# A spectral filter and a gated MLP on one core: the five engines' programs written without the block construct

## The chip, the cores and the metric

The kernel runs on one core of a Trainium2 chip. A core has five engines with an instruction queue each: TensorE (PE, with its weight loads listed as PEld), VectorE (DVE), ScalarE (ACT), GpSimd (POOL) and SyncE (SP, which here only issues transfers and waits). They run side by side and are held together by semaphores: an instruction can wait until a semaphore has reached a value, and raise one when it is done. The metric is the device time of one execution in microseconds (us); a shorter one is better.

## The reference

Layer norm of the input without scale or shift, then the sum of three parts: the input itself, a two-dimensional FFT filter, and a GELU-gated MLP.

```python
xn = _layernorm(x, axis=-1)                      # x: 1 x 2048 x 512, bf16
X  = rfft2(xn) * (w_r + 1j * w_i)                # filter of 2048 x 257
A  = irfft2(X, s=(2048, 512))
h  = gelu(xn @ w_gate) * (xn @ w_up)             # 512 -> 1792
B  = h @ w_down                                  # 1792 -> 512
out = x + A + B
```

## The kernel before, in words

The 2048 rows lie in 16 tiles of 128 rows in SBUF (`x_sb`). Each tile gets its statistics on DVE (`stats`), is normalised (`norm`) and transposed (`turn` on PE for the first ones, `turn_dma` by transposing transfers for the rest) into `xnT`. The MLP runs over four groups of four tiles and 14 chunks of 128 hidden columns: `gated` makes gate and up products in PSUM (`ps_gu`, L707), ACT evacuates them with GELU and a copy, DVE multiplies them into `hT` (L714), and `down` (L759) multiplies by `w_down` and adds the result to `x_sb`. The FFT filter is a chain of folded DFT products on PE (`ps_sp`) with butterflies on DVE between them, spread among the MLP's matmuls. For the last four tiles `down` comes at the very end; each is added on DVE (L770) and stored by a transfer of its own (`store`, L775), the last tile in two parts of 384 and 128 columns. The 17 stores are noted in `sch.finals`.

None of this is issued by hand. Every operation is registered in `_Sched` with its engine, an estimated cost, its reads and writes and a rank. `run` simulates the engines and fixes one order for each of them (`self.order`). `emit` then works out which waits each operation needs (`waits`), gives every engine one semaphore and every transfer one of its own, and writes the programs: `body(e, eng)` goes through one engine's list and, for each operation, issues its waits, the operation, and the increment of its semaphore. For SP it ends with a wait for each of the 17 stores (L327).

The change concerns only how `body` is called. In the kernel before this stands inside `with nc.Block() as block:` (L329), with a decorated function for each engine. The construct lets each engine jump from the common beginning of the program into a body of its own, and at the end lets each jump to a common last part, in which all engines drain their queues and meet: each of the four others reports to POOL on one semaphore, POOL waits for all four and then releases them on another. A wait that `body` asks for is put on the instruction that follows it, or becomes an instruction of its own where one has no room for more.

A meeting of the same kind stands at the beginning of every such program. It belongs to the `Bacc` object made in `kernel` (L1021), together with four small fills of constants on POOL, and lies outside of the construct.

Of the kernel before, what the change touches and what calls it, by code (L numbers as in the profile page):

```python
# [144 lines left out]
class _Sched:  # L145
# [123 lines left out]
    def emit(self, nc, es):  # L269
        sem = {e: es.enter_context(nc.semaphore("sem_" + e)) for e in self.ENGINES}  # L270
        cnt = {e: 0 for e in self.ENGINES}
        val = {}
        for e in self.ENGINES:
            for o in self.order[e]:
                if o.dma:
                    val[o] = (es.enter_context(nc.semaphore("dma%d" % o.seq)), 16, ("dma", o.seq))
                else:
                    cnt[e] += 1
                    val[o] = (sem[e], cnt[e], e)
        know = {}  # L280
        cur = {e: {} for e in self.ENGINES}
        waits = {}
        idx = {e: 0 for e in self.ENGINES}
        done = set()
        progress = True
        while progress:
            progress = False
            for e in self.ENGINES:
                while idx[e] < len(self.order[e]):
                    o = self.order[e][idx[e]]  # L290
                    if any(p not in done for p in o.preds):
                        break
                    need = []
                    c = cur[e]
                    for p in sorted((p for p, w in o.preds.items() if w), key=lambda p: -p.end):
                        s, v, n = val[p]
                        if c.get(n, 0) >= v:
                            continue
                        need.append((s, v, n))
                        for n2, v2 in know[p].items():  # L300
                            if c.get(n2, 0) < v2:
                                c[n2] = v2
                    best = {}
                    for s, v, n in need:
                        if n not in best or best[n][1] < v:
                            best[n] = (s, v)
                    waits[o] = list(best.values())
                    k = dict(c)
                    s, v, n = val[o]
                    k[n] = max(k.get(n, 0), v)  # L310
                    know[o] = k
                    done.add(o)
                    idx[e] += 1
                    progress = True
        assert all(idx[e] == len(self.order[e]) for e in self.ENGINES), "the orders of the engines form a circle"

        def body(e, eng):
            for o in self.order[e]:
                for s, v in waits[o]:
                    eng.wait_ge(s, v)  # L320
                ins = o.fn(eng)
                s, v, n = val[o]
                ins.then_inc(s, 16 if o.dma else 1)
            if e == "sp":
                for o in self.finals:
                    s, v, n = val[o]
                    eng.wait_ge(s, v)  # L327

        with nc.Block() as block:  # L329

            @block.sync
            def _(eng):
                body("sp", eng)

            @block.scalar
            def _(eng):
                body("act", eng)

            @block.vector
            def _(eng):  # L340
                body("dve", eng)

            @block.gpsimd
            def _(eng):
                body("pool", eng)

            @block.tensor
            def _(eng):
                body("pe", eng)


def bass_parallel_sum__spectral_gfnet__glu_gated_geglu__prompt_kernel(
# [683 lines left out]
```

## Time and profile before

| | us |
|---|---|
| median of 3 runs | 170.94 (170.75 to 171.29) |
| profiled execution, its own time | 171.11 |
| its span, first to last instruction of the program | 169.2 |
| PE busy (matmuls) | 165.7, 98% of the span |
| DVE busy | 145.9, 86% |
| ACT busy | 107.5, 64% |
| POOL busy | 10.5, 6% |

The span is counted from the first recorded instruction of the program, the drain of the opening meeting, to the end of its last, the release of the closing one. The execution's own time also holds what lies around the program, here 1.91 us. Instructions that only the sequencer of an engine handles (waits, drains, branches, the issuing of transfers) are marked with a q behind the engine's name and don't count as busy. In the listings by source line a row gives the engine, the operation and how often it ran, then the shortest, median and longest duration in ns, and the starts of the first and the last in us. "issue" is time in which an engine waited for nothing that the profile shows.

### The profile page before, as it was taken

The page shows a single profiled execution, that of the slowest core. Times are in us where ns is not written, and L with a number is a line of the kernel's source. Part 1 is how long each engine was busy: PE and PEld are TensorE (multiplying, and loading weights), DVE is VectorE, ACT ScalarE, POOL GpSimd, SP SyncE. Part 2 cuts the span into 40 slices and gives each one's busy share as a digit, 9 for nine tenths or more (in the row PEclk, how much of TensorE's full clock was granted, in tenths as well). Part 3 has the DMA queues.
Part 4 walks back from the last instruction along what each step waited for, and adds up shares of the span by engine and source line. Part 5 has one row for each costly group of instructions (what it writes and reads, how often), then busy time and mean ns, then how long its engine had stood idle before and what let it go on. Part 6 is the DMA issues. An engine that isn't in the chain of part 4 may idle for free.

```text
span 169.2 us, 2755 instructions
## 1 busy us (share of the span) xinstructions
PE 165.7 (98%) x1019; PEld 88.2 (52%) x1019; DVE 145.9 (86%) x294; ACT 107.5 (64%) x182; POOL 10.5 (6%) x25
## 2 busy tenths in 40 slices
PE   8999999999999999999999999999999999999994
PEld 3688884444554654344444446455444556544443
DVE  2785999997956399999999999999999995999932
ACT  3598887663975966669494739669556499761000
POOL 2030232520000000002000000000000000000000
PEclk9999999999999999999999999999999999999999
DMA  5999999995640625535000000000000000033311
GB/s 147 339 290 182 308 297 99 255 296 101 161 105 10 138 73 103 112 66 187 2 0 0 0 4 0 0 0 4 2 0 0 0 0 4 3 128 117 130 62 62
DMA packets 24927, 16.02 MB, mean 95 GB/s; under 512 B 10957, under 2 KB 24274, under 8 KB 24914
## 3 DMA queue, kind: packets, MB, share of 16 engines
q1 hardware_dynamic: 23714, 15.03, 37.3%
q10 hardware_dynamic: 1200, 0.82, 1.5%
q8 instruction: 8, 0.13, 0.3%
q14 instruction: 5, 0.04, 0.1%
HBM read 11.38 MB, written 2.10 MB: 80 GB/s over the span
## 4 chain that ended last, share of the span: by engine, by line
PE 93%; DMA 4%; DVE 1%; SPq 0%; issue 0%; DVEq 0%
PE ps_gu L707 54%; PE ps_dn L759 21%; PE ps_sp L759 7%; DMA xnT<-specB 2%; PE ps_sp L984 2%; PE ps_sp L615 2%; DMA x_sb<-in_A_x_dram 2%; PE ps_sp L843 2%; PE ps_gu L726 1%; PE ps_sp L924 1%; PE ps_sp L925 1%; PE ps_dn L726 1%; DVE bst L514 0%; PE ps_sp L847 0%; SPq L464 0%
## 5 line engine op out<-in xcount | busy, mean ns | idle before, releaser
L707 PE MATMUL ps_gu<-xnT,wg 128*128 128x512 bf16 (+1 forms) x252 | 57.1, 350 | 0.1
L707 PE MATMUL ps_gu<-xnT,wu 128*128 128x512 bf16 (+1 forms) x252 | 57.1, 350 | 0.0
L713 ACT ACTIVATE uu<-ps_gu 128x512 bf16<-128x512 f32 (+1 forms) x63 | 34.5, 547 | 12.6 <-PE ps_gu L707 11.5
L712 ACT ACTIVATE gg<-ps_gu 128x512 bf16<-128x512 f32 (+1 forms) x63 | 34.4, 550 | 11.3 <-PE ps_gu L707 9.7
L759 PE MATMUL ps_dn<-wd,hT 128*128 128x512 bf16 x168 | 39.2, 379 | 0.0
L707 PEld LDWEIGHTS ps_gu<-xnT,wu 128*128 128x128 bf16 x252 | 24.4, 98 | 21.5 <-ACT gg L712 0.2
L707 PEld LDWEIGHTS ps_gu<-xnT,wg 128*128 128x128 bf16 x252 | 24.3, 98 | 21.2 <-DMA xnT<-specB 0.4
L468 DVE TENSOR_TENSOR specB<-specB 128x512 bf16<-128x512 bf16 (+2 forms) x58 | 33.4, 610 | 0.7 <-ACT specB L989 0.5
L714 DVE TENSOR_TENSOR hT<-gg,uu 128x512 bf16<-128x512 bf16 (+1 forms) x63 | 23.6, 382 | 5.1 <-ACT uu L713 4.8
L759 PEld LDWEIGHTS ps_dn<-wd,hT 128*128 128x128 bf16 x168 | 16.1, 98 | 18.8 <-issue 0.4
L767 ACT ACTIVATE db<-ps_dn 128x512 bf16<-128x512 f32 x12 | 7.2, 597 | 17.5 <-PE ps_dn L759 17.5
L514 DVE BATCH_NORM_STATS2 bst<-x_sb 128x6 f32<-128x512 bf16 x16 | 10.9, 684 | 3.6 <-DMA x_sb<-in_A_x_dram 3.5
L468 DVE TENSOR_TENSOR specC<-specB 128x1024 bf16<-128x1024 bf16 (+2 forms) x18 | 12.6, 714 | 0.3
L759 PE MATMUL ps_sp<-wd,hT 128*128 128x512 bf16 (+2 forms) x70 | 12.3, 336 | 0.0
L468 DVE TENSOR_TENSOR specB<-specA 128x2048 bf16<-128x2048 bf16 x8 | 9.4, 1221 | 2.4 <-ACT specA L620 2.3
L759 PEld LDWEIGHTS ps_sp<-wd,hT 128*128 128x128 bf16 x70 | 6.3, 98 | 6.1 <-DVE x_sb L770 0.2
L468 DVE TENSOR_TENSOR specB<-specB,filt 128x2048 bf16<-128x2048 bf16 x8 | 9.4, 1223 | 0.0
L852 ACT ACTIVATE specA<-ps_sp 128x1024 bf16<-128x1024 f32 x8 | 7.9, 1039 | 1.3 <-PE ps_sp L843 1.3
L620 ACT ACTIVATE specA<-ps_sp 128x1024 bf16<-128x1024 f32 x8 | 7.9, 1029 | 0.3 <-PE ps_sp L615 0.3
L989 ACT ACTIVATE specB<-ps_sp 128x1024 bf16<-128x1024 f32 x8 | 8.0, 1038 | 0.0
L930 ACT ACTIVATE specC<-ps_sp 128x1024 bf16<-128x1024 f32 x8 | 7.8, 1043 | 0.0
L468 DVE TENSOR_TENSOR specA<-specB 128x2048 bf16<-128x2048 bf16 (+1 forms) x8 | 7.6, 986 | 0.1
(68 smaller groups left out, 122.0 us busy)
## 6 DMA issues: line engine op xcount, KB each, us to landing
out_dram<-x_sb SPq DMA_DIRECT2D x15, 128.0 KB, 1.8
wd<-in_B_w_down_dram SPq DMA_DIRECT2D x1, 1792.0 KB, 8.5
x_sb<-in_A_x_dram SPq DMA_DIRECT2D x3, 512.0 KB, 7.3
toki<-c_ti SPq DMA_DIRECT2D x1, 768.0 KB, 4.3
tokf<-c_tf SPq DMA_DIRECT2D x1, 576.0 KB, 4.1
x_sb<-in_A_x_dram SPq DMA_DIRECT2D x4, 128.0 KB, 3.7
wg<-in_B_w_gate_dram SPq DMA_DIRECT2D x2, 256.0 KB, 6.5
wu<-in_B_w_up_dram SPq DMA_DIRECT2D x2, 256.0 KB, 6.4
```

The lines of the kernel that those rows point to most:

```text
L468: return op("dve", c_tt(n), lambda e: e.tensor_tensor(o.ap, a.ap, b.ap, f), reads=(a, b), writes=(o,), key=key, **kw)
L514: op("dve", 0.61, lambda e: e.bn_stats(bst[:, s].ap, xs(s).ap), reads=(xs(s),), writes=(bst[:, s],), key=key, due=due, after=after)
L620: op("act", c_act(1024), lambda e, yv=yv, t=t: e.activation(yv.ap, spair(t).rearrange("p (s r i) -> p s i r", s=4, r=4), ACT.Copy), writes ...
L707: ins = e.matmul(gub(t, n), w.ap[:, dc, fc * P:(fc + 1) * P], xnT.ap[:, b, sl, dc, :], start=(dc == 0), stop=(dc == 3))
L712: op("act", c_act(n), lambda e: e.activation(gg.ap[:, gs.slot, 0:n], gub(g, n), ACT.Gelu_apprx_tanh), tiles=(g, gs), key=0.0)
L713: op("act", c_act(n), lambda e: e.activation(uu.ap[:, us.slot, 0:n], gub(u, n), ACT.Copy), tiles=(u, us), key=0.0)
L714: op("dve", c_tt(n), lambda e: e.tensor_tensor(hT.ap[:, h.slot, lo:lo + n], gg.ap[:, gs.slot, 0:n], uu.ap[:, us.slot, 0:n], MUL), tiles=(g ...
L759: ins = e.matmul(bank(), hT.ap[:, hs[(b, fc)].slot, sl * P:(sl + 1) * P], wd.ap[:, fc, lo:lo + n], start=(fc == 0), stop=(fc == NFC - 1))
L767: op("act", c_act(n), lambda e: e.activation(db.ap[:, d.slot, 0:n], bank(), ACT.Copy), tiles=(t, d), key=0.0)
L852: op("act", c_act(1024), lambda e, xv=xv, t=t: e.activation(xv.ap, spair(t), ACT.Copy), writes=(xv,), tiles=(t,), key=-0.5)
L930: op("act", c_act(1024), lambda e, gv=gv, t=t: e.activation(gv.ap, spair(t).rearrange("p (k x i) -> p k x i", k=4, x=4), ACT.Copy), writes ...
L989: op("act", c_act(1024), lambda e, rv=rv, t=t: e.activation(rv.ap, spair(t), ACT.Copy), writes=(rv,), tiles=(t,), key=-0.5)
```

## The change

The construct is gone. The five calls of `body` stand one after the other at the end of `emit`, each with the engine object itself, so that every engine's instructions go straight into the common stream of the program. No engine gets a body of its own to jump into, and there is no last part with drains and a meeting: each engine's program simply ends after its last instruction, SP's after the wait for the last of the 17 stores. Orders, waits, semaphores and the operations are those of before. The order of the calls (SP, ACT, PE, DVE, POOL) is the order in which the program is written, not one in which the engines run.

```diff
@@ -326,27 +326,8 @@
                     s, v, n = val[o]
                     eng.wait_ge(s, v)
 
-        with nc.Block() as block:
-
-            @block.sync
-            def _(eng):
-                body("sp", eng)
-
-            @block.scalar
-            def _(eng):
-                body("act", eng)
-
-            @block.vector
-            def _(eng):
-                body("dve", eng)
-
-            @block.gpsimd
-            def _(eng):
-                body("pool", eng)
-
-            @block.tensor
-            def _(eng):
-                body("pe", eng)
+        for e, eng in (("sp", nc.sync), ("act", nc.scalar), ("pe", nc.tensor), ("dve", nc.vector), ("pool", nc.gpsimd)):
+            body(e, eng)
```

## The prediction

> **What bounds the kernel now.** I read the page first: the engines' busy times, then the chain of work that ended last.
>
> ```profile
> span 169.2 us, 2755 instructions
> PE 165.7 (98%) x1019; PEld 88.2 (52%) x1019; DVE 145.9 (86%) x294; ACT 107.5 (64%) x182; POOL 10.5 (6%) x25
> ...
> PE 93%; DMA 4%; DVE 1%; SPq 0%; issue 0%; DVEq 0%
> ```
>
> TensorE (PE) is busy in 165.7 of 169.2 us, and 93% of the chain is its matmuls. The change touches no matmul, no transfer and no wait between them, so nearly all of the time is out of its reach. Two places can matter: the few tenths of a microsecond before the first instruction of `body`, and what follows the last matmul. For the second I read the chain of waits in order of time and then the timeline, both from 154 and 166 us on.
>
> ```profile
> 154.83 12.14 PE ps_sp L759 x70
> 166.97 0.02 issue
> 166.99 0.29 DVE x_sb L770
> ```
>
> ```profile
> 166.79 0.85 SPq L775 DMA_DIRECT2D out_dram<-x_sb  x2
> ```
>
> TensorE stops at 166.97. VectorE adds the last 128 columns until 167.28, and SyncE (SP) issues the last two stores, the second until 166.79 + 0.85 = 167.64. From there on only SP has something to wait for: the landing of the stores. Three answers of the trace show that end, line by line: L775 (the stores), L327 (SP's waits for them) and L329, which is the `with nc.Block()` line itself. The last of the three stands complete, with its drains.
>
> ```profile
> L775 SPq DMA_DIRECT2D out_dram<-x_sb x2: 332/332/333, 166.8 to 167.3; - x2
> ...
> DMA to landing us min/median/max: 1.4/1.5/1.6
> ```
>
> ```profile
> L327 SPq EVENT_SEMAPHORE  x8: 28/28/28, 167.7 to 168.8; - x8
> ```
>
> ```profile
> L329 POOLq EVENT_SEMAPHORE  x2: 17/17/17, 169.1 to 169.1; - x2
> L329 POOLq DRAIN  x1: 647/647/647, 79.8 to 79.8; - x1
> L329 ACTq DRAIN  x1: 627/627/627, 154.9 to 154.9; - x1
> L329 PEldq DRAIN  x1: 1622/1622/1622, 165.4 to 165.4; - x1
> L329 DVEq DRAIN  x1: 330/330/330, 167.0 to 167.0; - x1
> L329 SPq COMPARE_BRANCH  x1: 41/41/41, 168.8 to 168.8; - x1
> L329 SPq DRAIN  x1: 13/13/13, 169.0 to 169.0; - x1
> L329 SPq EVENT_SEMAPHORE  x1: 17/17/17, 169.2 to 169.2; - x1
> L329 ACTq EVENT_SEMAPHORE  x1: 17/17/17, 169.2 to 169.2; - x1
> L329 DVEq EVENT_SEMAPHORE  x1: 21/21/21, 169.2 to 169.2; - x1
> L329 PEldq EVENT_SEMAPHORE  x1: 51/51/51, 169.2 to 169.2; - x1
> ```
>
> The columns are shortest, median and longest duration in ns, and the starts of the first and last of the group in us. The last store is issued at 167.3 and lands after 1.4 us, at 168.7. SP's last wait on L327 follows at 168.8. Then comes what the construct itself adds: SP's branch at 168.8, its drain at 169.0, the message from GpSimd (POOL) at 169.1, and the five engines' release at 169.2. The other four engines have drained before 167.4 (167.0 + 0.33 for VectorE is the latest) and wait for SP alone.
>
> **The change, part by part.**
>
> *The meeting at the end* goes: five drains and six semaphore instructions. PE's, ACT's, DVE's and POOL's drains end before 167.4, under the landing of the stores (168.7), so taking them away gives nothing; their cover is that landing, and if the stores were done earlier PE's drain would end at 165.4 + 1.62 = 167.0, still earlier. SP's drain, the two messages of POOL and the releases are on the path, from 169.0 to 169.2.
>
> *SP's branch* goes. It is the only COMPARE_BRANCH on that line; the other engines show none. It starts at 168.8, and SP's next instruction starts at 169.0, so it holds the path for about 0.2 us though its own record is 41 ns. The program waits for 17 stores: eight wait instructions on L327 carry two each, so the 17th wait sits on the branch. Without the branch that wait needs an instruction of its own, one more row of L327 at 28 ns.
>
> So the removed stretch is 169.2 − 168.8 = 0.4 us, less 0.03 us for the wait that replaces the branch: **−0.37 us**. Rounding in the rows makes it −0.27 to −0.47.
>
> [...]
>
> *The entry into the blocks* goes too. Here are the meeting that opens the program (L1021, made with the `Bacc` object and kept by the change) and the first instructions of `body`.
>
> ```profile
> L1021 SPq EVENT_SEMAPHORE  x1: 17/17/17, 0.6 to 0.6; - x1
> L1021 ACTq EVENT_SEMAPHORE  x1: 17/17/17, 0.6 to 0.6; - x1
> L1021 DVEq EVENT_SEMAPHORE  x1: 21/21/21, 0.7 to 0.7; - x1
> L1021 PEldq EVENT_SEMAPHORE  x1: 51/51/51, 0.7 to 0.7; - x1
> ```
>
> ```profile
> 0.72 0.10 POOL L503 MEMSET eps<- 128x1 f32 x1 [0.29 <-POOLq L1021]
> 0.72 0.36 ACTq L464 DMA_DIRECT2D smallc<-c_small  x1
> 0.72 2.73 SPq L464 DMA_DIRECT2D x_sb<-in_A_x_dram  x4
> 0.73 0.14 PEld L477 LDWEIGHTS ps_dn<-const-bfloat16-1.0 128*128 128x128 bf16 x2 [0.73 <-issue]
> ```
>
> SP, ACT and PE leave that meeting at 0.6 to 0.7 and start their first work at 0.72 to 0.73. Between those lies at most 0.12 us, which is what any two instructions of a queue are apart here (SP's eight waits on L327 cover 1.1 us, most of it real waiting). No branch of the kind seen at the end fits, since that one took 0.2. I therefore cost the entry at nothing; its bounds are a gain of 0.1 (all of that gap) and a loss of 0.1 (a first instruction that starts one such gap later).
>
> What a shift of the start would do is seen in the chain's beginning, where the transfer of x follows SP's second issue. A shift of SP alone would pass on through that piece.
>
> ```profile
> 1.17 3.14 DMA x_sb<-in_A_x_dram
> ```
>
> *The order of the instructions* on each queue does not change: `body` runs over the same lists with the same waits. Nothing is moved past anything, and POOL's and ACT's last instructions (80 and 155 us) are followed by less, with nobody waiting for them.
>
> *What lies around the span.* The profiled execution took 171.11 us against a span of 169.2, so 1.91 us lie outside of it. No row shows what they hold. The nearest price is the meeting on L1021, from the first drain at 0.0 to the releases at 0.7:
>
> ```profile
> L1021 SPq DRAIN  x1: 7/7/7, 0.0 to 0.0; - x1
> ...
> L1021 POOLq DRAIN  x1: 173/173/173, 0.3 to 0.3; - x1
> ```
>
> If the way out holds something of that kind, four engines that arrive early could do their part ahead; the gain is at most the whole 0.7 us, and 0.2 us if only one release (169.0 to 169.2 on L329) is saved. It can as well be a loss, up to the 0.37 gained, if the program's end was waited for in two places and the second now takes the time of the first. I take 0, the middle, and keep both ends.
>
> **Sum.** Profiled execution: 171.11 − 0.37 = 170.74. It was 0.17 above the median of the three runs (170.94), so the median to expect is 170.94 − 0.37 = **170.57 us**, a change of 0.22%. About 0.3%, 0.51 us, is what a measurement of this kernel can tell from no change.
>
> **The rivals.**
>
> *The engines that come early shorten the way out as well.* For it: POOL is done at 80.4 and ACT at 155.5 (154.9 + 0.63), yet both are held until 169.2. Against: their work outside the span isn't seen. Time: 170.94 − 0.37 − 0.2 = 170.37, at most 170.94 − 0.37 − 0.7 = 169.87.
>
> *The meeting only moves.* Whatever closes an execution must also know that all engines are done, so the wait that L329 ends comes back outside the span, and 1.91 us becomes 2.28. For it: 1.91 us is room for such a thing. Against: SP is free 0.37 earlier, and it comes last either way. Time: 170.94.
>
> [...]
>
> *One instruction fetch of PE comes late (slower).* The packets by queue, and PE's costliest group (its last number is PE's idle time ahead of the group, in us):
>
> ```profile
> q8 instruction: 8, 0.13, 0.3%
> ...
> L707 PE MATMUL ps_gu<-xnT,wg 128*128 128x512 bf16 (+1 forms) x252 | 57.1, 350 | 0.1
> ```
>
> Eight packets of 16 KB took 0.3% of 16 engines' span, 0.003 · 16 · 169.2 / 8 = 1.0 us each. If a straight stream puts its boundaries elsewhere and a fetch is asked for after PE has run out, PE stands for up to 1.0 us and the chain passes all of it on: 170.94 − 0.37 + 1.0 = 171.57. It decides from a delay of 0.37 us on. Against: the group's 252 matmuls, spread over most of the span, show 0.1 us of idle time, so eight such fetches are hidden now, and PE's queue of 2 · 1019 weight loads and matmuls becomes shorter by only two instructions.
>
> *The branch into a block costs a fetch now.* An entry that empties what was fetched would cost one such packet, 1.0 us, and the change would give 170.94 − 0.37 − 1.0 = 169.57. The gap of at most 0.12 us at the start speaks against it. [...]
>
> **How the numbers follow.** The forecast has 0.47. Its centre, 170.57, lies 0.14 above the bound for faster (170.43), and the three runs shown lie up to 0.35 from their median, so I count 0.19 of it as faster and 0.28 as the same. The early engines have 0.24: 0.22 faster, 0.02 the same. The moved meeting has 0.12, the same. The late fetch has 0.14, slower. The branch's fetch has 0.03, faster. So faster 0.19 + 0.22 + 0.03 = 0.44, the same 0.28 + 0.02 + 0.12 = 0.42, slower 0.14.
>
> The range reaches down to the early engines' bound, 169.87, and up past the moved meeting's 170.94 by 0.2 for the runs' own scatter, to 171.15; the late fetch and the branch's fetch, together 0.17, lie outside. The forecast's own range, by the rounding (±0.1) and the scatter (±0.2), is 170.27 to 170.87.
>
> **What would show each step.** In the profile after: no row of L329's kind and no COMPARE_BRANCH; nine waits of SP for the stores instead of eight, the last at 168.8, and a span of 168.8 to 168.9. The first transfers still at 0.72, the 70 matmuls of the last stage still starting at 154.8 and ending at 167.0: entry and middle unmoved. The time outside the span, 171.11 − 169.2 before, tells the first two rivals apart: below 1.7 the early engines pay, near 2.28 the meeting has moved. Idle time of PE in the middle, with the last stage starting later than 155, would be the late fetch. The prediction is wrong if the last stage moves at all, or if the time outside the span takes up the difference.

## The result, and the profile after

The changed kernel takes 170.38 us (median of 18 runs, 170.07 to 170.61); the kernel before, run beside it, 171.25 (18 runs, 170.61 to 172.36). The ratio is 0.9946, with a 95% interval of 0.9932 to 0.9961: faster. The fall of 0.5% is above the 0.3% that the prediction took as the least that can be told from no change. A later comparison of the same two programs gave 170.32 against 170.93, a ratio of 0.9963 (0.9948 to 0.9977).

The page of the profile after, its first lines and the shares of the chain that ended last:

```profile
span 168.8 us, 2732 instructions
PE 164.3 (97%) x1007; PEld 88.1 (52%) x1019; DVE 145.7 (86%) x294; ACT 107.5 (64%) x182; POOL 10.4 (6%) x25
...
PE 93%; DMA 4%; DVE 1%; issue 1%; SPq 0%; DVEq 0%
```

The bound is where it was. Of the 1019 matmuls twelve have no record in this trace (the weight loads are complete). Where one is missing, the chain shows a piece of about 0.05 us as "issue", which explains the higher share of "issue" and part of PE's lower busy time. Another part is in waits early on, for DVE 0.8 us in place of 0.3 and for a transfer 0.2 us; the last stage starts no later for them. The changed source is 19 lines shorter, so L759 is now L740, L770 is L751 and L775 is L756. The start, in the timeline from 0.7 us on:

```profile
0.72 0.37 ACTq L445 DMA_DIRECT2D smallc<-c_small  x1
0.72 0.10 POOL L484 MEMSET eps<- 128x1 f32 x1 [0.29 <-POOLq L1002]
0.72 0.40 SPq L445 DMA_DIRECT2D x_sb<-in_A_x_dram  x1
0.73 0.14 PEld L458 LDWEIGHTS ps_dn<-const-bfloat16-1.0 128*128 128x128 bf16 x2 [0.73 <-issue]
```

ACT, POOL, SP and PE begin at 0.72 to 0.73, as before. DVE's first instruction comes at 3.1 in both, so its entry can't be read. The last stage, in the chain in order of time (start, duration), then the stores in the timeline, and SP's waits for them:

```profile
154.87 7.77 PE ps_sp L740 x36
162.64 0.05 issue
162.70 4.31 PE ps_sp L740 x33
167.01 0.02 issue
167.03 0.29 DVE x_sb L751
```

```profile
166.84 0.84 SPq L756 DMA_DIRECT2D out_dram<-x_sb  x2
```

```profile
L327 SPq EVENT_SEMAPHORE  x9: 17/28/28, 167.7 to 168.8; - x9
```

The stage starts at 154.87 (154.83 before) and its last addition at 167.03 (166.99). There are nine waits instead of eight, the last still at 168.8, and behind it nothing: no branch, no drain, no message, no release. The span ends there, at 168.8 instead of 169.2.

The profiled execution took 170.52 us, so 170.52 − 168.8 = 1.7 us lie outside the span, against 1.9 before. This second difference is no accident of one execution. Each run gives its time and its span, and over 18 runs of the changed kernel the time outside is 1.62 to 1.75 us, mean 1.67; over 35 runs of the kernel before it is 1.82 to 1.92, mean 1.87. The spans scatter far more (168.6 to 170.8 in those 35 runs), so the mean time outside can be read to a few hundredths where a median of the times can't.

### The profile page after: what moved, and what is told of

Its sections match the earlier page's. It is cut to its first block, busy times and chain, and to the rows that moved or that the text cites. A ratio compares the mean times of both kernels' runs of the same rounds, so it can differ in the third digit from the quotient of the medians.

```text
span 168.8 us, 2732 instructions
## 1 busy us (share of the span) xinstructions
PE 164.3 (97%) x1007; PEld 88.1 (52%) x1019; DVE 145.7 (86%) x294; ACT 107.5 (64%) x182; POOL 10.4 (6%) x25
## 4 chain that ended last, share of the span: by engine, by line
PE 93%; DMA 4%; DVE 1%; issue 1%; SPq 0%; DVEq 0%
PE ps_gu L688 54%; PE ps_dn L740 21%; PE ps_sp L740 7%; DMA xnT<-specB 2%; PE ps_sp L596 2%; PE ps_sp L965 2%; PE ps_sp L824 2%; DMA x_sb<-in_A_x_dram 2%; PE ps_gu L707 1%; PE ps_sp L905 1%; PE ps_sp L906 1%; PE ps_dn L707 1%; DVE bst L495 0%; PE ps_sp L828 0%; SPq L445 0%
## 5 line engine op out<-in xcount | busy, mean ns | idle before, releaser
L740 PE MATMUL ps_dn<-wd,hT 128*128 128x512 bf16 x157 | 36.8, 379 | 0.7 <-issue 0.2
L740 PEld LDWEIGHTS ps_dn<-wd,hT 128*128 128x128 bf16 x168 | 16.1, 98 | 19.1 <-DMA wd<-in_B_w_down_dram 0.5
L740 PE MATMUL ps_sp<-wd,hT 128*128 128x512 bf16 (+2 forms) x69 | 12.2, 336 | 0.1
L740 PEld LDWEIGHTS ps_sp<-wd,hT 128*128 128x128 bf16 x70 | 6.3, 98 | 6.1 <-DVE x_sb L751 0.2
```

The source lines that it names most:

```text
L740: ins = e.matmul(bank(), hT.ap[:, hs[(b, fc)].slot, sl * P:(sl + 1) * P], wd.ap[:, fc, lo:lo + n], start=(fc == 0), stop=(fc == NFC - 1))
```

## The experiments

Two numbers carry them. One is the time outside the span, as a mean over the runs. The other is the stretch from the start of the last store's issue to the end of the span, taken from the trace's own records. It leaves out the scatter of everything earlier.

| kernel | last store's issue to end of span, us | outside the span, us | median, us | ratio to before (95%) |
|---|---|---|---|---|
| before | 1.93 | 1.87 | 170.90 | |
| e1 before again | 1.92 | 1.87 | 170.81 | 0.9984 (0.9963 to 1.0005) |
| e3 no branch | 1.80 | 1.88 | 170.71 | 0.9983 (0.9962 to 1.0004) |
| e2 meeting only | 1.74 | 1.89 | 170.74 | 0.9987 (0.9963 to 1.0011) |
| e9 after again | 1.48 | 1.67 | 170.32 | 0.9963 (0.9948 to 0.9977) |
| e4 all four held | 1.52 | 1.81 | 170.48 | 0.9976 (0.9951 to 1.0001) |
| e5 ACT held | 1.48 | 1.82 | 170.36 | 0.9968 (0.9951 to 0.9986) |
| e6 PE held | 1.52 | 1.94 | 170.53 | 0.9987 (0.9971 to 1.0002) |
| e7 DVE held | 1.49 | 1.40 | 169.98 | 0.9940 (0.9916 to 0.9965) |
| e8 POOL held | 1.48 | 2.20 | 170.69 | 0.9977 (0.9961 to 0.9993) |
| e10 drain at DVE's end | 1.49 | 1.31 | 169.79 | 0.9947 (0.9926 to 0.9968) |
| e11 DVE waits for the stores | 1.51 | 1.40 | 169.92 | 0.9946 (0.9930 to 0.9963) |
| e12 drain at DVE's start | 1.49 | 1.30 | 169.82 | 0.9926 (0.9898 to 0.9953) |

The first row is the original profile with the 35 runs beside e1 to e4. In the other comparisons the median of before was 170.90 (e5 to e8), 170.93 (e9 to e11) and 171.00 (e12); e1 to e11 ran on one chip, e12 on another.

### e1: the kernel before once more

No edit.

> The kernel before once more, unchanged, so that every run has its span beside its time. The theory of the end (the construct costs 0.4 us in the span, from SP's branch to the release, and 0.2 us outside of it, because engines that are held until the end can't do their part of the way out early) expects 1.9 us outside the span in every run (1.7 after the change), a span about 0.4 us longer than after, and a ratio to the kernel before of 1.000. The rival of the start or the middle (the entry into the blocks sometimes costs a fetch) expects spans that scatter by more than the 0.5 us (168.4 to 168.9) seen after the change, since the runs of before reach from 170.61 to 172.36.

The time outside is 1.87 (1.83 to 1.91), the stretch at the end 1.92, the ratio 0.9984 with 1.000 inside its interval. Its spans reach from 168.5 to 169.3, those of the kernel before beside it to 170.8. Spans of this width come in other variants too: e2's reach from 168.3 to 170.1, and e2 has no blocks. Over all runs with a span on record, the span lies more than 0.7 us above the median of its kind in 6 of 111 with the blocks and in 4 of 107 without (every kernel without blocks taken together). So the long spans are no sign of the blocks, and the rival of the start finds no support here.

### e2: the meeting without the blocks

```diff
         for e, eng in (("sp", nc.sync), ("act", nc.scalar), ("pe", nc.tensor), ("dve", nc.vector), ("pool", nc.gpsimd)):
             body(e, eng)
+        nc.all_engine_barrier()
```

> The changed kernel with the meeting of all engines put back at its end, without blocks and without SP's branch. The theory of the end expects a span about 0.2 us above the changed kernel's (drain, two messages, release) and 1.9 us outside it, so about 0.4 us above the changed kernel and 0.2 us below before (ratio 0.999). If entry and branch cost nothing and only the meeting counts, the time is that of before (1.000). If the blocks' entry or layout is what costs, it is that of the changed kernel (0.995 to 0.996).

SP's part of the meeting and POOL's messages, by source line, after nine waits on L327:

```profile
L327 SPq EVENT_SEMAPHORE  x9: 17/28/28, 167.7 to 168.7; - x9
```

```profile
L331 POOLq EVENT_SEMAPHORE  x2: 17/17/17, 168.8 to 168.9; - x2
...
L331 PEldq DRAIN  x1: 1622/1622/1622, 165.4 to 165.4; - x1
...
L331 SPq DRAIN  x1: 13/13/13, 168.8 to 168.8; - x1
L331 SPq EVENT_SEMAPHORE  x1: 17/17/17, 169.0 to 169.0; - x1
```

The last wait is at 168.7, the release at 169.0. The stretch at the end is 1.74, so the meeting alone is 1.74 − 1.48 = 0.26 us of the span. The time outside is 1.89, as with blocks. PE's drain of 1.62 us is there as before and ends at 167.0, long ahead of SP.

### e3: no branch for SP

```diff
                 for o in self.finals:
                     s, v, n = val[o]
                     eng.wait_ge(s, v)
+                eng.drain()
 
         with nc.Block() as block:
```

> The kernel before with one more drain on SP behind its 17 waits, still inside its block: the 17th wait then sits on the drain, and nothing is left that needs a branch of its own. The theory of the end expects that no COMPARE_BRANCH is recorded, that the stretch from the last wait to the meeting's drain shrinks by 0.1 to 0.15 us, and a ratio of 0.999. If the 0.2 us at that place is not the branch but the jump into the common last part, the time stays that of before (1.000).

SP's last rows by source line (L328 is the added drain, L330 the block):

```profile
L328 SPq DRAIN  x1: 13/13/13, 168.5 to 168.5; - x1
```

```profile
L330 SPq DRAIN  x1: 7/7/7, 168.6 to 168.6; - x1
L330 SPq EVENT_SEMAPHORE  x1: 17/17/17, 168.8 to 168.8; - x1
```

There is no COMPARE_BRANCH any more. From SP's step with the 17th wait to the meeting's drain it is now 0.07 us instead of 0.18, and the whole stretch shrinks from 1.92 to 1.80. The branch is a real cost, 0.11 to 0.12 us more than an ordinary step; in the profile before its record is 41 ns and the step from it to the next instruction 0.18 us. In these traces it is recorded only where a wait sits on it: with the wait elsewhere SP goes from its block into the common part with no branch on record, as the other engines do. The 0.12 us can't be told from the scatter in the ratio (0.9983, 0.9962 to 1.0004); they are read from the stretch.

### e4: all four engines held to the end

```diff
             if e == "sp":
                 ...
+            else:
+                s, v, n = val[self.finals[-1]]
+                eng.wait_ge(s, v)
```

> The changed kernel in which ACT, PE, DVE and POOL each end with a wait for the last store, so that all five engines end within 0.1 us of each other as in the kernel before, yet without drains, messages or blocks. The theory that early engines shorten the way out expects the changed kernel's span (168.4 to 168.9) with 1.9 us outside it, so 0.2 us above the changed kernel (ratio 0.996 to 0.997). If the 0.2 us outside come from the drains or the meeting itself, the time outside stays at 1.7 and the ratio at 0.995.

The four added waits, by source line, in an execution whose last stage started 1.5 us later than usual:

```profile
L330 ACTq EVENT_SEMAPHORE  x1: 17/17/17, 170.3 to 170.3; - x1
L330 POOLq EVENT_SEMAPHORE  x1: 17/17/17, 170.3 to 170.3; - x1
L330 DVEq EVENT_SEMAPHORE  x1: 21/21/21, 170.3 to 170.3; - x1
L330 PEldq EVENT_SEMAPHORE  x1: 51/51/51, 170.3 to 170.3; - x1
```

All five engines end together at 170.3, the end of that span. Outside lie 1.81 us (1.75 to 1.86), between the two values and nearer to that of before. That looked like the early engines paying.

This execution also shows where a long span can come from. PE waits for DVE where the changed kernel's PE goes on without a wait at 102.2:

```profile
103.45 0.23 PE L908 MATMUL ps_sp<-toki,specA 128*128 128x128 bf16 x1 [0.80 <-DVE specA L875]
```

The chain that ended last leads from there back over DVE and POOL to a transfer of the filter, which lands at 81.0; POOL's work on it began at 81.2 here, and at 78.8 in the changed kernel's first profile. By that chain, 0.80 of the 1.5 us come from a filter that landed late. A late last stage with PE idle, the prediction's sign of a late instruction fetch, came here without the blocks, and this wait was for data, not for a fetch.

### e5 to e8: one engine held at a time

The same wait in one engine's program alone.

```diff
+            elif e == "act":        # e5; "pe", "dve", "pool" in e6, e7, e8
+                s, v, n = val[self.finals[-1]]
+                eng.wait_ge(s, v)
```

> The changed kernel with ACT alone held at its end until the last store has landed; the other three engines end early. With all four held the time outside the span was 1.82 us instead of 1.67. If every engine's way out is the same and SP is merely the last, one engine more at the end changes nothing: 1.67 us. If one engine has a longer way out than SP, holding that one alone gives 1.82 us. For ACT, whose waits take as long as SP's (17 ns), I expect 1.67.

> The same with PE alone held until the last store. PE's waits take 51 ns where the others' take 17 to 28, so if a slower engine's way out sets the end, PE is the likeliest: 1.82 us outside the span. If it is another engine, or the number of engines that come late, it stays at 1.67 or lies between.

> The same with DVE alone held. If DVE's way out is the longer one, 1.82 us outside the span, else 1.67. In the changed kernel DVE ends at 167.3, 1.5 us ahead of SP, so a longer way out would be covered there.

> The same with POOL alone held. POOL is the engine that the others report to in the kernel's own meetings; if it plays that part on the way out as well, holding it costs what holding all costs, 1.82 us outside the span; else 1.67.

Against 1.67 with none held, the time outside is 1.82 with ACT held, 1.94 with PE, 2.20 with POOL, and 1.40 with DVE. ACT's 1.82 is the value that was named for it but not expected; the other three are none of the values named. Two of the four can't come from lateness alone. Holding one engine can't make the rest end earlier, yet DVE's hold takes 0.27 us off. And holding POOL alone costs 0.53 us where holding POOL and three more costs 0.14. Whatever ends an execution, it is not simply the last engine to arrive.

### e9: the changed kernel again, beside the next two

No edit.

> The changed kernel once more beside the others, on the chip of the experiments. The theory of the end expects 1.67 us outside the span as in its first runs (1.62 to 1.75), against 1.87 for before, and a span 0.2 to 0.4 us shorter than before's: in all a ratio of 0.996 to 0.998. If the 0.92 us between the two first medians came from the construct and not from the scatter of the runs of before, the ratio is 0.995 or below.

Outside 1.67 again; the stretch at the end 1.48 again. The ratio is 0.9963, and the medians differ by 170.93 − 170.32 = 0.61 us. The first comparison's medians differ by 171.25 − 170.38 = 0.87 us (the expectation has 0.92 by a slip). The two sizes differ mainly on the side of before, with a median of 171.25 there and 170.93 here and single runs up to 172.36 there; the spans of those first 18 runs aren't at hand, so the cause of that is not shown.

### e10: one drain at the end of DVE's program

```diff
+            elif e == "dve":
+                eng.drain()
```

> The changed kernel with one drain at the end of DVE's program. DVE then has as many instructions as when it was held until the last store (1.40 us outside the span, less than the 1.67 of the changed kernel), but it still ends early, at about 167.3. If being late is what shortened the way out, 1.67 us. If it is only where DVE's program ends among its fetched instructions, 1.40.

DVE's drain by source line:

```profile
L329 DVEq DRAIN  x1: 330/330/330, 166.7 to 166.7; - x1
```

DVE ends at 167.0, 1.5 us ahead of SP, and the time outside falls to 1.31 us (1.27 to 1.34). So it is not lateness that shortened the way out in e7: an early DVE with one instruction more does the same, and takes off 0.09 us more.

### e11: DVE waits for the stores in SP's place

```diff
-            if e == "sp":
+            if e == "dve":
                 for o in self.finals:
```

> The changed kernel in which DVE instead of SP waits for the 17 stores; SP ends with the issue of the last one, 1.1 us earlier. The span should stay within 0.1 us of the changed kernel's, since the last wait still follows the landing. If a late DVE is what shortens the way out, 1.40 us outside the span or less, and a ratio of about 0.995 to before on the same chip. If the way out needs SP to be last as well, it goes back to 1.67 or above.

The waits, now DVE's:

```profile
L327 DVEq EVENT_SEMAPHORE  x9: 21/49/50, 166.7 to 168.5; - x9
```

A wait for two stores takes DVE 49 ns where it took SP 28; the stretch at the end is 1.51. Outside lie 1.40 us, the value of e7. DVE's program has nine instructions more than the changed kernel's here, one more in e7, and SP's has nine fewer. So eight more instructions on DVE, a shorter program on SP and an SP that ends 1.2 us ahead of DVE leave the time outside, taken together, where e7 had it. What each of them does by itself was not separated.

### e12: the same drain at the start of DVE's program

```diff
         def body(e, eng):
+            if e == "dve":
+                eng.drain()
             for o in self.order[e]:
```

> The changed kernel with the same one drain on DVE, now ahead of DVE's first instruction, where DVE has nothing to do until 3 us. DVE's program is as long as with the drain at its end (1.31 us outside the span, against 1.67 without), but its last instruction is again the addition on L751. If the number of instructions is what counts, or where DVE's program ends among the fetched ones, 1.3 to 1.4 us outside the span. If it counts that something of the sequencer's own follows DVE's last addition, 1.67. A value far from both would say that the time around the span is a matter of the whole program and of no single ending.

The drain's row:

```profile
L319 DVEq DRAIN  x1: 10/10/10, 0.7 to 0.7; - x1
```

It takes 10 ns at 0.7 us, where DVE has nothing to do, and its last instruction is the addition once more. The time outside is 1.30 us (1.28 to 1.36), the same as with the drain at the end, though on another chip. So it doesn't matter whether the drain is DVE's last instruction; that there is a drain more in DVE's program does. In both runs DVE ends at 167.0. When DVE ends may still count for the 0.09 us between e10 and e7. Whether it is the number of DVE's instructions or the place in the fetched instructions at which its program ends, which the expectation puts side by side, was not separated.

The medians of e10 and e12, 169.79 and 169.82 us, lie below that of e9, 170.32. The intervals of e10's and e9's ratios overlap, so the medians alone don't show a gain over the changed kernel. Of the 0.53 us between e10 and e9, on the same chip, 0.36 lie outside the span (1.67 − 1.31), and these are shown by the steady time outside. The rest is put down to scatter of the spans, since the two programs' stretches at the end are equal to 0.01 us.

## Why the prediction was right or wrong

The time was 170.38 against 170.57, inside the range, and on the side of the forecast: faster. The change was clear, where the forecast put it just short of that. That the time came within 0.19 us is in part luck: the forecast was a fall of 0.37 us from 170.94, the median of three runs, while the medians measured side by side fell by 0.87 and 0.61 us. Point by point:

*The bound and the middle.* Right. The last stage starts within 0.05 us of where it did, and PE's, DMA's and DVE's shares of the chain are the same. PE's fetch did not come late in this execution: by the prediction's estimate the stage would have started up to 1.0 us later.

*The entry into the blocks, costed at nothing.* Right for ACT, POOL, SP and PE: first instructions at 0.72 to 0.73 on both sides, with 0.08 us between SP's release and its first transfer in both. The rival in which the entry costs a fetch falls with it. At the entry no branch is recorded at all; the only COMPARE_BRANCH of the kernel before is SP's, at 168.8.

*The meeting at the end.* Right in mechanism and place. PE's, ACT's, DVE's and POOL's drains end before the last store lands and cost nothing in the span; SP's drain, the messages and the release cost 0.26 us (e2).

*SP's branch.* Right that it held the path: 0.18 us from the branch to the next instruction, of which 0.11 is the branch's own (e3).

*The wait that takes the branch's place.* Mis-sized. The prediction added 0.03 us for a 17th wait behind the other eight. It came first instead: the single wait (17 ns, the shortest of the nine) is at 167.7, under the landing of the last store, and the wait for the last store is the last of the nine. So the whole step of 0.07 us went. The sum in the span is 1.92 − 1.48 = 0.44 us, as 0.11 for the branch, 0.07 for the step and 0.26 for the meeting, where the prediction had 0.37 with 0.27 to 0.47 as bounds.

*What lies around the span.* This is the term that failed: it was taken as 0 and is −0.20 us (1.87 to 1.67). With it the sum is 0.44 + 0.20 = 0.64, against 0.61 between the medians of e9 and its kernel before. The rival of the early engines gave 170.37, and 170.38 was measured; the sign that the prediction set for it, below 1.7 us outside the span, was met too. Its reason is not borne out. For DVE, e7, e10 and e12 speak against it: with DVE early or late, the time outside falls by a single instruction more. For ACT, PE and POOL, whose holds add 0.15, 0.27 and 0.53 us, the lateness and the added wait were not separated; that all four holds together add only 0.14 us fits no simple sum of either. That the meeting only moves, the other rival, is out, as the time outside fell (1.87 to 1.67); its premise, that whatever closes an execution must know of all engines, was an assumption of the prediction that no row shows.

*What stays open.* Why the time outside goes by the program. It is the same in every comparison of one program (1.87, 1.87 and 1.85 for before on one chip, 1.86 on the other; 1.67 twice for the changed kernel), and between 1.30 and 2.20 for programs that differ from the changed kernel by a single added instruction. A late engine may have a part in it as well: e7 (late) is 0.09 above e10 (early) with as many instructions, though of another kind. e2 shows that the meeting without blocks has the time outside of before. Whether that is its eleven extra instructions or its holding of the engines was not separated. Where a program's end falls among its fetched instructions, an idea that the expectations of e10 and e12 name, was not tested by itself. No instruction of these traces is recorded outside the span. So of the gain, the 0.44 us in the span are explained by the rows, and the 0.20 us outside of it are measured but not explained.

## What to carry to other kernels

A closing meeting of all engines and a branch with a wait on it cost what follows the last arrival, here 0.26 and 0.11 us; the other engines' drains, up to 1.62 us long, cost nothing here, since they ended before the last store landed. The step into an engine's own block cost nothing where it could be read. Where tenths of a microsecond count, compare the span and the time outside of it apart from each other, over all runs: the mean of the second came back within about 0.02 us for one program, and moved by up to 0.53 us when a single instruction was added, more than the 0.44 us that the change took off the span. So a gain there doesn't prove the idea of the edit.

## What was not expected

The time outside the span depends on the program in a way that no argument from the trace foresaw. One drain of 10 ns at the start of DVE's program takes 0.37 us off (1.67 to 1.30, e12, on another chip); one wait at the end of POOL's adds 0.53 (e8); the same wait on all four engines adds 0.14 (e4).

In these traces a branch is recorded only where a wait sits on it. The other engines' jumps into and out of their blocks, and SP's own once its wait sits on a drain (e3), leave no record; at the entry, and for SP in e3, they take no time that shows either.
